# Two VectorE passes, with POOL and ScalarE exchanged, in the conversion of doubles to float32

## The chip, the cores and the metric

The kernel runs on one core of a Trainium2 chip. A core has TensorE (PE, with PEld for its weight loads), VectorE (DVE), ScalarE (ACT), GpSimd (POOL) and SyncE (SP), which here issues the DMAs. The metric is the time on the device, in microseconds. Before the change it is 1098.83 us, the median of 3 runs (1097.06 to 1099.32). 0.2% of that is about 2.2 us.

## The reference

Three layers follow one another: an attention with a compressive memory, and two feed-forward layers ("MoE" in the names, with one expert each).

```
scores = q @ k.T / sqrt(D), causal, softmax          B=4, H=8, S=576, D=64
local  = softmax @ v
mem    = (phi(q) @ M_prev) / (phi(q) @ z_prev + 1e-6)      phi(x) = elu(x) + 1
x      = g * mem + (1 - g) * local                   g = sigmoid(beta)
x      = (h * cos(h)) @ w_out,  h = x @ w_in         2304 tokens, 512 -> 2048 -> 512
out    = (h * tanh(softplus(h))) @ w_out,  h = x @ w_in
```

The weights of the feed-forward layers reach the kernel as doubles, two 32-bit words for each number, and are made into float32 on the core.

## The kernel before, in words

Attention runs over 16 pairs of heads (4 batches by 4 pairs), each in five steps of up to 128 queries: scores on TensorE, mask and minimum on VectorE (line 248), exponential on ScalarE (251), the scaling by the row's sum on POOL (274), transposes (306) and the product with v (333). MoE 1's first half (its first 1024 hidden columns) is done on blocks of 256 tokens as soon as a batch has left attention, interleaved with the next batch; its second half follows on blocks of 512 tokens, and then MoE 2. Line 429 is the first product of a feed-forward unit, lines 487 and 496 the second product. Between them stand, for the cosine layer, lines 376, 377, 381 and 384 (ScalarE, VectorE, ScalarE, VectorE) on pairs of hidden tiles, and the split of the result into a rounded part and a rest (lines 113 to 117 and 401). Every product is made of three, of such rounded parts and rests.

The weights come in 64 pieces of 128 x 512 numbers, sixteen for each half of a layer (four groups of two pieces from w_in and two from w_out). A piece goes through `to_f32`: a DMA on the SP queue loads 512 KB into one of two staging buffers (wst), ScalarE and POOL each work on one of the words, three VectorE passes (lines 127, 128, 131) put the float32 together, and `load_half` rounds it (`scaled("wh", ...)`, ScalarE and POOL in turn) and subtracts (line 161, VectorE and POOL in turn). Only then is the staging buffer free for another load. The words of one number lie side by side, so every pass on a word reads or writes with a step of two.

The first sixteen pieces are converted beside attention's first batch (the loop that calls `converted`), the next sixteen (`gb`) and a further sixteen (`gc`) during MoE 1, the last (`gd`) while MoE 2 begins. The engine of many steps is given by the table `TURNS`; in which order the instructions stand on each engine and on the SP queue is set by a scheduler from the priorities and its own estimates of durations, so a changed step can move its neighbours too. Each engine and the SP queue work through their instructions in the order so set: one that waits holds those behind it. The loads of x for a feed-forward block (xbH, xbL, line 474) go through the same SP queue as the loads of wst (line 123).

Of the kernel before, what the change touches and what calls it, by code (L numbers as in the profile page):

```python
# [9 lines left out]
F32 = mybir.dt.float32  # L10
F32R = mybir.dt.float32r
I32 = mybir.dt.int32
U32 = mybir.dt.uint32
AF = mybir.ActivationFunctionType
ALU = mybir.AluOpType
# [16 lines left out]

TURNS = dict(
    sc0="p", ql0="vp", kh0="a", kl0="vp", qh0="a", aT0="a",
    sc="p", ql="vp", kh="p", kl="ppv", ws="p", w0l="pv", w1l="vp", w2l="vp", w3l="vp", gl="p", gh="v", bh="a", mh="a",
    wh="ap", aT="av", yl="p", ml="vp", y0="v", y1="a", qh="a", aD="v",
)

# [1 line left out]
REBIAS = 2.0 ** -112  # L40
# [3 lines left out]
def attention_moe_moe_kernel(  # L44
# [14 lines left out]
    nc = tc.nc  # L59
    P = 128  # L60
# [21 lines left out]
    const = ctx.enter_context(tc.tile_pool(name="const"))  # L82
# [13 lines left out]
    nc.vector.reciprocal(gate, igate)  # L96
    nc.vector.tensor_scalar(omg, gate, -1.0, 1.0, ALU.mult, ALU.add)

    c_seven = const.tile([P, 1], F32, name="c_seven")
    nc.gpsimd.memset(c_seven, 7.0)  # L100

    counts = {}

    def turn_of(kind, first=False):
        kind += "0" if first else ""
        n = counts.get(kind, 0)
        counts[kind] = n + 1
        return {"a": nc.scalar, "p": nc.gpsimd, "v": nc.vector}[TURNS[kind][n % len(TURNS[kind])]]

    def scaled(kind, dst, src, scale=1.0, first=False):  # L110
        eng = turn_of(kind, first)
        if eng is nc.scalar:
            eng.activation(dst, src, AF.Copy, scale=scale)  # L113
        elif scale == 1.0 and eng is nc.vector:
            eng.tensor_copy(dst, src)
        else:
            eng.tensor_scalar(dst, src, scale, 1.0, ALU.mult, ALU.mult)  # L117

    def to_f32(src, dst=None):


        st = wk.tile([P, SM, 2], I32, tag="wst", name="wst", bufs=BUFS["wst"])
        nc.sync.dma_start(st, src)
        lo, hi = st[:, :, 0], st[:, :, 1]
        scaled("ws", hi.bitcast(F32), hi.bitcast(F32), REBIAS)
        nc.scalar.activation(lo, lo.bitcast(U32), AF.Relu, scale=-(2.0 ** -29), bias=c_seven)  # L126
        nc.vector.scalar_tensor_tensor(lo, hi, 3, lo, ALU.logical_shift_left, ALU.bitwise_or)  # L127
        nc.vector.tensor_scalar(hi, hi, -(1 << 31), 7, ALU.bitwise_and, ALU.bitwise_or)  # L128
        if dst is None:
            dst = lo  # L130
        nc.vector.tensor_tensor(dst, lo, hi, ALU.bitwise_xor)  # L131
        return dst.bitcast(F32)

    def weight_pieces(win, wout, half, tl):
# [30 lines left out]
    def from_double(win, wout, half):  # L165
        def f(tl):
            for src in weight_pieces(win, wout, half, tl):
                yield to_f32(src)
        return f
# [505 lines left out]
```

## Time and profile before

| | |
|---|---|
| median of 3 runs | 1098.83 us |
| the profiled execution, device time | 1098.41 us |
| its span | 1096.6 us |
| TensorE busy | 1056.2 us |
| VectorE busy | 517.7 us |
| ScalarE busy | 472.7 us |
| POOL busy | 428.4 us |
| mean granted TensorE clock (1 is 2.4 GHz, 0.5 is 1.2 GHz) | 0.978 |

Times in the rows count from the start of the span. The roughly 1.8 us between the span and the device time lie around it. A busy time is the time in which an engine had an instruction; it includes what an instruction waited for while it ran. TensorE's instructions overlap and their ends are modelled. The chain of waits is found by going back from the last instruction, at each step to what released it. A "waits" row says who waited for whom, in how many places, and how long the longest was.

### The profile page before, as it was taken

To read this page: it belongs to the slowest core of one execution; us is meant where nothing else is said; L and a number is where in the kernel's file an instruction comes from. 1 tells how busy PE (TensorE), PEld (TensorE's weight loads), DVE (VectorE), ACT (ScalarE), POOL (GpSimd) and SP (SyncE) were. 2 spreads that over 40 slices of the span, in tenths; PEclk is the share of its full clock that TensorE was granted. 3 is DMA by queue.
4 is the path that set the end of the run, shared out by engine and by line. 5 is a ranking of instruction groups with operands and counts; after the bars stand their busy time and mean duration, and the time that the engine had idled before them with its cause. 6 is when DMAs were issued, how large, how long until landed. Compare 5 with 4: busy or idle time off the path is not lost.

```text
span 1096.6 us, 17569 instructions
## 1 busy us (share of the span) xinstructions
PE 1056.2 (96%) x6672; PEld 903.1 (82%) x6672; DVE 517.7 (47%) x1246; ACT 472.7 (43%) x947; POOL 428.4 (39%) x454
## 2 busy tenths in 40 slices
PE   6889899999999999999999999999999999999998
PEld 4767688888888899987777888988888888888897
DVE  7999885647474657655785232656200000000000
ACT  6776475637373633334454343543421222232231
POOL 5987563425242424455576333454211101010100
PEclk8998799999999999999999999999999999999999
DMA  6565442414131265333455432643300210110010
GB/s 214 184 193 189 141 145 66 140 59 138 60 95 35 80 221 182 122 114 125 165 200 183 144 116 77 218 139 97 129 6 1 77 39 0 58 39 1 20 39 20
DMA packets 66373, 117.04 MB, mean 107 GB/s; under 512 B 5616, under 2 KB 25072, under 8 KB 66288
## 3 DMA queue, kind: packets, MB, share of 16 engines
q1 hardware_dynamic: 66288, 115.91, 32.1%
q8 instruction: 53, 0.87, 0.3%
q14 instruction: 32, 0.26, 0.1%
HBM read 87.58 MB, written 28.31 MB: 106 GB/s over the span
## 4 chain that ended last, share of the span: by engine, by line
PE 70%; DVE 11%; DMA 7%; ACT 5%; POOL 4%; issue 3%; SPq 0%; ACTq 0%; POOLq 0%; DVEq 0%
PE h L429 29%; PE y L496 18%; PE y L487 12%; PE o L333 3%; PE tp L306 3%; PE sp L246 3%; DMA wst<-in_w1i_dram 2%; DVE wst L127 2%; DMA wst<-in_w1o_dram 2%; DVE wst L131 2%; DMA wst<-in_w2o_dram 1%; PE o L322 1%; DVE wst L128 1%; DMA wst<-in_w2i_dram 1%; DVE w L161 1%
## 5 line engine op out<-in xcount | busy, mean ns | idle before, releaser
L429 PE MATMUL h<-xbH,w 128*128 128x256 f32 (+1 forms) x1536 | 398.0, 340 | 8.0 <-DVE u L384 5.2
L429 PEld LDWEIGHTS h<-xbH,w 128*128 128x128 f32 x1536 | 268.1, 190 | 43.7 <-DVE u L384 6.9
L429 PE MATMUL h<-xbL,w 128*128 128x256 f32 (+1 forms) x768 | 259.3, 338 | 0.2 <-DMA xbL<-xsL 0.2
L487 PE MATMUL y<-g,w 128*128 128x256 f32 (+1 forms) x1344 | 224.8, 321 | 2.1 <-POOL g L401 1.2
L487 PEld LDWEIGHTS y<-g,w 128*128 128x128 f32 x1344 | 195.8, 195 | 24.3 <-issue 3.3
L496 PE MATMUL y<-w,g 128*128 128x512 f32 x864 | 201.8, 389 | 0.0
L496 PEld LDWEIGHTS y<-w,g 128*128 128x128 f32 x864 | 162.0, 188 | 33.4
L401 DVE TENSOR_TENSOR g<-e,g 128x512 fp32r<-128x512 f32 x36 | 25.3, 702 | 288.9 <-ACT g L113 258.3
L429 PEld LDWEIGHTS h<-xbL,w 128*128 128x128 f32 x768 | 146.1, 190 | 15.9 <-DMA xbL<-xsL 0.8
L401 POOL TENSOR_TENSOR g<-e,g 128x512 fp32r<-128x512 f32 x36 | 47.7, 1325 | 276.4 <-ACT g L113 276.4
L401 POOL TENSOR_TENSOR g<-u,g 128x512 fp32r<-128x512 f32 x72 | 95.9, 1347 | 122.0 <-ACT g L113 64.7
L274 POOL TENSOR_SCALAR at<-at,sm,omg 128x128 f32<-128x128 f32 (+2 forms) x144 | 108.4, 762 | 87.7 <-DVE sm L272 60.7
L393 ACT ACTIVATE e<-h 128x512 f32<-128x512 f32 x72 | 42.8, 594 | 216.6 <-PE h L429 216.2
L126 ACT ACTIVATE wst<-wst,c_seven 128x512 int32<-128x512 uint32 x64 | 49.3, 772 | 96.5 <-DMA wst<-in_w2o_dram 32.2
L127 DVE SCALAR_TENSOR_TENSOR wst<-wst 128x512 int32<-128x512 int32 x64 | 54.2, 847 | 68.1 <-POOL wst L117 34.4
L251 ACT ACTIVATE at<-at,mn 128x128 f32<-128x128 f32 (+3 forms) x128 | 71.0, 555 | 32.1 <-DVE mn L248 29.7
L377 DVE SCALAR_TENSOR_TENSOR u<-u,h 128x512 f32<-128x512 int32 x72 | 49.0, 682 | 61.7 <-ACT u L376 61.7
L376 ACT ACTIVATE u<-h 128x512 int32<-128x512 f32 x72 | 41.8, 591 | 80.9 <-PE h L429 72.3
L306 PE MATMUL tp<-ident,at 128*128 128x128 f32 x384 | 67.2, 294 | 8.0 <-DVE xL L338 3.1
L117 POOL TENSOR_SCALAR wst<-wst 128x512 f32<-128x512 f32 x64 | 46.9, 733 | 71.1 <-DMA wst<-in_w2o_dram 18.9
L333 PE MATMUL o<-aT,vt 128*64 128x128 f32 (+1 forms) x896 | 65.0, 276 | 0.0
L248 DVE CUSTOM_DVE_ANT_0 at<-sp,mask 128x128 f32<-128x128 f32 (+3 forms) x128 | 58.9, 481 | 10.7 <-PE sp L246 9.9
(94 smaller groups left out, 1244.9 us busy)
## 6 DMA issues: line engine op xcount, KB each, us to landing
wst<-in_w1i_dram SPq DMA_DIRECT2D x16, 512.0 KB, 3.8
wst<-in_w1o_dram SPq DMA_DIRECT2D x16, 512.0 KB, 4.1
wst<-in_w2i_dram SPq DMA_DIRECT2D x16, 512.0 KB, 3.7
wst<-in_w2o_dram SPq DMA_DIRECT2D x16, 512.0 KB, 3.6
qd<-in_qT_dram SPq DMA_DIRECT2D x16, 320.0 KB, 3.3
vt<-in_vn_dram SPq DMA_DIRECT2D x16, 320.0 KB, 3.3
xbH<-xsH SPq DMA_DIRECT2D x20, 256.0 KB, 4.7
xbL<-xsL SPq DMA_DIRECT2D x20, 256.0 KB, 4.7
```

Source lines behind the costliest of these rows:

```text
L126: nc.scalar.activation(lo, lo.bitcast(U32), AF.Relu, scale=-(2.0 ** -29), bias=c_seven)
L127: nc.vector.scalar_tensor_tensor(lo, hi, 3, lo, ALU.logical_shift_left, ALU.bitwise_or)
L248: nc.vector.tensor_tensor_reduce(at[:, :N], sp[:, :N], mask[:, SM - q0:SM - q0 + N], SSC, 3.0e38, ALU.add, ALU.min, mn[:, j:j + 1])
L251: marks["act"] = nc.scalar.activation(at[:, :N], at[:, :N], AF.Exp, bias=mn[:, j:j + 1], scale=-1.0, accum_out=sm[:, j:j + 1]).ins
L274: turn_of("sc", b == 0).tensor_scalar(at[:, :N], at[:, :N], sm[:, j:j + 1], gates[j], ALU.mult, ALU.mult)
L306: nc.tensor.transpose(tp[:, c:c + P], at[:, c:c + P], ident)
L333: marks["pe"] = nc.tensor.matmul(o[j * D:(j + 1) * D, :n], st["vt"][:kk, c, j * D:(j + 1) * D], a, start=False, stop=c == i, skip_group_ch ...
L377: nc.vector.scalar_tensor_tensor(u, u.bitcast(I32), -TWO_PI, h, ALU.mult, ALU.add)
L401: turn_of(kind).tensor_tensor(gL, g, gH.bitcast(F32), ALU.subtract)
L429: nc.tensor.matmul(h[:, a * T:(a + 1) * T], w_[:, c, f0:f0 + P], x_[c], start=m == 0, stop=m == 3 * NC - 1)
L487: nc.tensor.matmul(y[e // per][:, cols], w_[:, f, es], g_, start=fst and m == 0 and e % per == 0, stop=lst and m == 2, skip_group_check=True)
L496: nc.tensor.matmul(y[t], g_[:, tsl], w_[:, f, :], start=fst and m == 0, stop=lst and m == 2, skip_group_check=True)
```

## The change

Before, POOL multiplies the upper word (read as float32) by 2^-112 in place, ScalarE turns the lower word into 7 minus its top three bits (rounded, by a Relu that keeps it at 0 or more), and VectorE makes three passes: shift the upper word and OR the lower one in, take the sign of the upper word and OR 7 to it, and XOR the two. After, POOL turns the lower word into its top three bits, held at 7 at most, as they are and not subtracted from 7, with integers in and out; ScalarE multiplies the upper word by 2^-112 in a Copy; and VectorE makes two passes: shift and OR as before, then take the sign of the upper word and OR it to the result. The constant of seven and the entry "ws" of the table go.

```diff
-    sc="p", ql="vp", kh="p", kl="ppv", ws="p", w0l="pv", w1l="vp", w2l="vp", w3l="vp", gl="p", gh="v", bh="a", mh="a",
+    sc="p", ql="vp", kh="p", kl="ppv", w0l="pv", w1l="vp", w2l="vp", w3l="vp", gl="p", gh="v", bh="a", mh="a",
...
-    c_seven = const.tile([P, 1], F32, name="c_seven")
-    nc.gpsimd.memset(c_seven, 7.0)
...
         lo, hi = st[:, :, 0], st[:, :, 1]
-        scaled("ws", hi.bitcast(F32), hi.bitcast(F32), REBIAS)
-        nc.scalar.activation(lo, lo.bitcast(U32), AF.Relu, scale=-(2.0 ** -29), bias=c_seven)
+        nc.gpsimd.tensor_scalar(lo, lo.bitcast(U32), 2.0 ** -29, 7.0, ALU.mult, ALU.min)
+        nc.scalar.activation(hi.bitcast(F32), hi.bitcast(F32), AF.Copy, scale=REBIAS)
         nc.vector.scalar_tensor_tensor(lo, hi, 3, lo, ALU.logical_shift_left, ALU.bitwise_or)
-        nc.vector.tensor_scalar(hi, hi, -(1 << 31), 7, ALU.bitwise_and, ALU.bitwise_or)
         if dst is None:
             dst = lo
-        nc.vector.tensor_tensor(dst, lo, hi, ALU.bitwise_xor)
+        nc.vector.scalar_tensor_tensor(dst, hi, -(1 << 31), lo, ALU.bitwise_and, ALU.bitwise_or)
```

Line numbers behind the change are lower by three (from line 99 on) and by four (from line 128 on): lines 127 and 131 of before are 124 and 127 of after, line 377 is 373, 384 is 380, 161 is 157, 474 is 470 and 123 is 120.

On VectorE, the first piece in the first batch of attention, before the change. `at<-sp,mask` and `mn` are the mask and minimum of a step, `mo` the memory's result, `kl` and `ql` the rests of k and q, `ph` phi(q):

```order
L127 SCALAR_TENSOR_TENSOR wst<-wst 128x512
L291 TENSOR_TENSOR mo<-mp,den 128x256
L212 TENSOR_TENSOR kl<-kd,kh 128x576
L248 ISA at,mn<-sp,mask 128x512
L248 ISA mn 128x1
L224 TENSOR_SCALAR ph<-qt 128x576
L128 TENSOR_SCALAR wst<-wst 128x512
L262 ISA at,mn<-sp,mask 128x512
L262 ISA mn 128x1
L213 TENSOR_TENSOR ql<-qd,qh 128x640
L131 TENSOR_TENSOR wst<-wst 128x512
```

And the same place after it:

```order
L124 SCALAR_TENSOR_TENSOR wst<-wst 128x512
L286 RECIPROCAL den<-den 128x4
L244 ISA at,mn<-sp,mask 128x512
L244 ISA mn 128x1
L208 TENSOR_TENSOR kl<-kd,kh 128x576
L127 SCALAR_TENSOR_TENSOR wst<-wst 128x512
L244 ISA at,mn<-sp,mask 128x512
L244 ISA mn 128x1
L287 TENSOR_TENSOR mo<-mp,den 128x256
L220 TENSOR_SCALAR ph<-qt 128x576
L258 ISA at,mn<-sp,mask 128x512
```

The first pass on the piece has moved ahead of a step's mask, the last one ahead of the next; between the first and the last lie four rows where there were nine, and the other rows keep their order but for one (`mo`).

On VectorE in the first blocks of MoE 1's second half, before (`u` is the tile of the cosine's steps, `w<-wst,w` the rest of a piece):

```order
L377 SCALAR_TENSOR_TENSOR u<-u,h 128x512
L127 SCALAR_TENSOR_TENSOR wst<-wst 128x512
L377 SCALAR_TENSOR_TENSOR u<-u,h 128x512
L128 TENSOR_SCALAR wst<-wst 128x512
L131 TENSOR_TENSOR wst<-wst 128x512
L384 TENSOR_TENSOR u<-h,u 128x512 x2
L127 SCALAR_TENSOR_TENSOR wst<-wst 128x512
L161 TENSOR_TENSOR w_6530<-wst,w_6529 128x512
L128 TENSOR_SCALAR wst<-wst 128x512
L131 TENSOR_TENSOR wst<-wst 128x512
```

After:

```order
L373 SCALAR_TENSOR_TENSOR u<-u,h 128x512 x2
L124 SCALAR_TENSOR_TENSOR wst<-wst 128x512
L380 TENSOR_TENSOR u<-h,u 128x512 x2
L127 SCALAR_TENSOR_TENSOR wst<-wst 128x512
L124 SCALAR_TENSOR_TENSOR wst<-wst 128x512
L127 SCALAR_TENSOR_TENSOR wst<-wst 128x512
L157 TENSOR_TENSOR w_6494<-wst,w_6493 128x512
L373 SCALAR_TENSOR_TENSOR u<-u,h 128x512 x2
```

The two passes that make `u` from `h` stand together where a first pass on a piece stood between them, and each piece has one row less.

On the SP queue in the same part of the program, before (`xbH` and `xbL` are blocks of x, `wst` pieces of weights):

```order
L123 DMA wst<-in_w2i_dram 128x2x512 x2
L123 DMA wst<-in_w2o_dram 128x1024 x2
L474 DMA xbH<-xsH 128x2x512
L474 DMA xbL<-xsL 128x2x512 x2
L474 DMA xbH<-xsH 128x2x512
L123 DMA wst<-in_w2i_dram 128x2x512 x2
L522 DMA ysH<-yh 128x512 x2
```

After:

```order
L120 DMA wst<-in_w2i_dram 128x2x512
L120 DMA wst<-in_w2o_dram 128x1024 x2
L470 DMA xbL<-xsL 128x2x512
L470 DMA xbH<-xsH 128x2x512
L120 DMA wst<-in_w2i_dram 128x2x512
L470 DMA xbL<-xsL 128x2x512
L470 DMA xbH<-xsH 128x2x512
L120 DMA wst<-in_w2i_dram 128x2x512
L120 DMA wst<-in_w2o_dram 128x1024
```

The four loads of x stood together; now a load of weights stands between the first two and the last two.

## Rows read from the trace of the kernel before

**Rows 1.** Page, part 1: busy time of each engine
```profile
...
PE 1056.2 (96%) x6672; PEld 903.1 (82%) x6672; DVE 517.7 (47%) x1246; ACT 472.7 (43%) x947; POOL 428.4 (39%) x454
...
```

**Rows 2.** Windows: stretch, length, busy of PE, PEld, DVE, ACT, POOL; clock, DMA
```profile
...
0.00:165.00 165.00, 140.87 (x1132) 112.65 (x1133) 146.35 (x455) 110.06 (x296) 117.66 (x151) 0.90 0.56 178
165.00:412.00 247.00, 243.72 (x2129) 217.84 (x2129) 145.18 (x465) 127.46 (x290) 90.59 (x108) 0.98 0.31 100
412.00:585.00 173.00, 163.98 (x998) 145.02 (x997) 118.29 (x175) 72.93 (x108) 96.19 (x90) 0.99 0.46 152
...
700.00:790.00 90.00, 90.00 (x420) 75.50 (x419) 45.38 (x61) 36.38 (x59) 41.46 (x40) 1.00 0.37 118
...
```

**Rows 3.** Windows, same columns, hundred microseconds of the first stage
```profile
...
20.00:120.00 100.00, 87.28 (x715) 69.14 (x715) 95.77 (x289) 69.87 (x196) 80.50 (x84) 0.87 0.59 187
...
```

**Rows 4.** Groups, shapes apart: instructions | busy us, mean ns | idle before
```profile
...
L131 DVE TENSOR_TENSOR wst<-wst 128x512 int32<-128x512 int32 x64 | 57.1, 897 | 0.7
L127 DVE SCALAR_TENSOR_TENSOR wst<-wst 128x512 int32<-128x512 int32 x64 | 54.2, 847 | 68.1 <-POOL wst L117 34.4 <-ACT wst L126 30.2 <-ACT e L393 2.8
...
L126 ACT ACTIVATE wst<-wst,c_seven 128x512 int32<-128x512 uint32 x64 | 49.3, 772 | 96.5 <-DMA wst<-in_w2o_dram 32.2 <-DMA wst<-in_w2i_dram 26.4 <-DMA wst<-in_w1o_dram 21.2
...
L117 POOL TENSOR_SCALAR wst<-wst 128x512 f32<-128x512 f32 x64 | 46.9, 733 | 71.1 <-DMA wst<-in_w2o_dram 18.9 <-DMA wst<-in_w1i_dram 18.2 <-DMA wst<-in_w2i_dram 17.2
...
L161 POOL TENSOR_TENSOR w<-wst,w 128x512 fp32r<-128x512 f32 x32 | 45.8, 1432 | 7.8 <-ACT w L113 6.3
...
L128 DVE TENSOR_SCALAR wst<-wst 128x512 int32<-128x512 int32 x64 | 37.5, 593 | 0.7
...
L113 ACT ACTIVATE w<-wst 128x512 fp32r<-128x512 f32 x32 | 21.5, 671 | 28.8 <-DVE wst L131 28.8
...
```

**Rows 5.** Tile wst: duration min/median/max in ns, first and last start us
```profile
...
L117 POOL TENSOR_SCALAR wst<-wst x64: 638/667/1197, 9.9 to 770.3; 128x512 f32<-128x512 f32 x64
...
L127 DVE SCALAR_TENSOR_TENSOR wst<-wst x64: 659/694/1800, 16.3 to 771.1; 128x512 int32<-128x512 int32 x64
L128 DVE TENSOR_SCALAR wst<-wst x64: 407/426/1545, 19.2 to 771.8; 128x512 int32<-128x512 int32 x64
L131 DVE TENSOR_TENSOR wst<-wst x64: 665/693/1793, 21.7 to 772.3; 128x512 int32<-128x512 int32 x64
...
```

**Rows 6.** Windows, line 128 alone: stretch, length, busy (instructions), clock, DMA
```profile
...
0.00:165.00 165.00, 8.23 (x16) 0.90 0.56 178
...
412.00:585.00 173.00, 15.88 (x29) 0.99 0.46 152
...
700.00:790.00 90.00, 8.06 (x14) 1.00 0.37 118
...
```

**Rows 7.** Chain that ended last, shares by line, of 20 to 120
```profile
...
by line: issue 9.9%; DVE wst L131 8.1%; PE o L333 7.0%; POOL at L274 6.6%; PE tp L306 6.6%; DVE at L248 6.5%; DVE wst L127 5.4%; DMA wst<-in_w1o_dram 4.4%; DVE ph L226 3.8%; DMA wst<-in_w1i_dram 3.6%; DVE w L161 3.4%; DVE wst L128 3.4%; POO
...
```

**Rows 8.** Chain that ended last, shares by line, of 412 to 600
```profile
...
by line: DMA wst<-in_w1i_dram 8.3%; DMA wst<-in_w2o_dram 7.6%; issue 7.5%; DMA wst<-in_w2i_dram 6.6%; DVE wst L127 6.1%; POOL g L401 5.6%; DMA wst<-in_w1o_dram 5.4%; PE h L429 4.9%; DVE wst L131 4.8%; DVE u L384 4.5%; DVE wst L128 4.4%; DVE
...
```

**Rows 9.** Waits of TensorE, 412 to 600: total us, times, longest
```profile
...
PE h L429 <- DVE u L384: 5.2, 4, 2.3
PE h L429 <- DMA xbH<-xsH: 2.0, 1, 2.0
PE y L487 <- POOL g L401: 1.2, 4, 0.6
PE y L487 <- DVE g L115: 0.9, 1, 0.9
```

**Rows 10.** Waits of the SP queue, 412 to 600, same columns
```profile
...
SPq L123 <- DVE wst L131: 67.9, 13, 8.3
...
```

**Rows 11.** Timeline, 569 to 587: start, length, instruction, [idle before, releaser]
```profile
...
575.11 5.60 SPq L123 DMA_DIRECT2D wst<-in_w2o_dram  x2
...
580.80 0.39 SPq L474 DMA_DIRECT2D xbH<-xsH  x1
...
585.39 0.50 PE L429 MATMUL h<-xbH,w 128*128 128x512 f32 x1 [2.00 <-DMA xbH<-xsH]
...
```

## The prediction

> **What bounds the kernel now.** I read the busy times first, then the windows by stage, then the chain of waits in the two stages that looked unfilled, and at last the waits of TensorE and of the SP queue there. TensorE is busy for 1056.2 of 1096.6 us [rows 1], so the first question is where the other forty lie and where "busy" hides a slow pace. From 700 to 790 it is busy for 90.00 of 90 us [rows 2], although fourteen pieces are converted there [rows 6]: nothing that VectorE saves in that stretch reaches the end. From 165 to 412 it is busy for 243.72 of 247 us, and only two pieces fall there. What is left is the first 165 us (attention, with the first sixteen pieces of weights beside it) and the stretch from 412 to 600 (MoE 1 with the next two half sets).
>
> In the first stretch TensorE is busy for 140.87 us at a mean granted clock of 0.90, POOL for 117.66, VectorE for 146.35 of 165 [rows 2]. From 20 to 120 VectorE is busy for 95.77 of 100 us [rows 3]: it is the engine with no slack. The chain of waits agrees: the lines of the conversion on VectorE (131, 127, 128) hold 8.1%, 5.4% and 3.4% of these 100 us [rows 7].
>
> From 412 to 600 VectorE has slack, but the conversion is a chain of its own: a load, ScalarE and POOL side by side, three VectorE passes, the cast and the subtraction, and only then is one of the two staging buffers free again. The loads of wst, lines 126, 127, 128 and 131 and the steps after them fill much of that stretch's chain [rows 8]. TensorE itself waits little: 5.2 us on line 384, 2.0 us on an xbH load, 1.2 and 0.9 us on the split of g, 9.3 us together [rows 9]. The xbH wait is the SP queue's doing: its issues of wst waited 67.9 us on line 131 [rows 10], and the xbH load left at 580.80, just behind two wst issues that together span 5.60 us, for a matmul that waited until 585.39 [rows 11].
>
> **The change, part by part.** All against the profiled execution: span 1096.6 us, device time 1098.41, which is 0.4 us under the median of the runs, 1098.83; the two can be used for each other.
>
> 1. Line 128 goes: 64 passes, 593 ns mean, 37.5 us of VectorE [rows 4]. In the first stage these are 16 passes and 8.23 us [rows 6]. Lower end of the gain: what the chain shows, 3.4% of 100 us = 3.4 us [rows 7]. Upper end: all 8.2 us, because an engine without slack passes on everything behind it. VectorE is near the second case but not the only member of the chain; I take 5.5. What comes late next is POOL's scaling in line 274 (6.6% of the chain) and TensorE's own transposes and products [rows 7].
>
> 2. Line 131 turns from TENSOR_TENSOR into SCALAR_TENSOR_TENSOR, the form that line 127 has: 897 ns before, 847 ns for the form [rows 4]. Their medians are 693 and 694 ns [rows 5], so the difference of means is waiting, not work. Taken as 0, ends -0.8 and +0.8 us for sixteen pieces at 0.05.
>
> 3. ScalarE's step becomes a scaled copy. The same engine's copy with the same strided input is 671 ns, the step with the bias tile is 772 [rows 4]: 0.1 us less, 1.6 us in the first stage, where ScalarE has slack. VectorE's line 127 waited 30.2 us on it in all, mostly later. Taken as 0.5, ends 0 and 1.6.
>
> 4. POOL's step reads unsigned integers, multiplies, takes a minimum and writes integers. No row shows POOL on integers. The nearest row is POOL's one-input pass of the same size and stride, 733 ns [rows 4], 638 at its least [rows 5]; the farthest that is plausible is POOL's two-input pass on the same tile, 1432 ns [rows 4]. The passes are alike in inputs, elements and stride, so I take 733 and a cost of 0; ends: 1.5 us gained (16 x 0.095) and 11.2 us lost (16 x 0.70) in the first stage.
>
> 5. From 412 to 600 the removed passes hold 4.4% of 188 us = 8.3 us of the chain [rows 8], but TensorE can only give back what it waits: 5.2 + 2.0 = 7.2 us in the waits that hang on VectorE and on the SP queue [rows 9]. Each of these five waits has at least one removed pass ahead of it, 0.55 us on average (15.88 over 29 [rows 6]): 2.7 us; a staging buffer that is free sooner adds a little for xbH. I take 3.5, ends 0 and 7.2.
>
> 6. From 700 to 790 another 8.06 us of passes go [rows 6]: 0, since TensorE covers them. It would cost something only if TensorE had a gap there, and it has none.
>
> The order of work is made anew. In the first stage the first piece's two passes stand within six rows of VectorE where its three stood within eleven; from 412 on the two passes of line 377 stand side by side more often, where a conversion pass that waited for its load stood between them. On SP, two loads of weights move behind or between the loads of x. I cost this at 0 on the whole, with rival three for its bad side.
>
> Sum: 5.5 + 0.5 + 3.5 = 9.5 us, so 1098.4 - 9.5 = 1088.9, said as 1089. The ends together: 8.2 + 0.8 + 1.6 + 1.5 + 7.2 = 19.3 gained gives 1079; 3.4 - 0.8 = 2.6 gained gives 1096, and POOL's bad end comes on top as a rival.
>
> One thing speaks for more than this. Line 128 takes 407 ns at the least and 1545 at the most, and line 131 from 665 to 1793 [rows 5], so passes of fixed size wait for something while they run. The Trainium skill, "SBUF — State Buffer", section "Who interferes with whom", says that VectorE and GpSimd share one pair of SBUF ports as an exclusive lock, taken for a whole instruction by whichever starts first. By that rule each removed pass would also stop holding up POOL, up to 16 x 0.43 = 6.9 us of POOL in the first stage, an estimate that I leave out of the sum because POOL has slack there; these durations agree with the rule without proving it.
>
> **Rivals.**
>
> Slow POOL (slower). If the new POOL pass costs what the two-input pass costs, 1432 ns, each piece gains 0.51 us on VectorE and loses 0.70 on POOL, and line 127 already waited 34.4 us on that POOL step [rows 4]. First stage 16 x 0.19 = 3.0 us lost; from 412 to 600 half of 29 x 0.15 = 2.2 us lost; 1103.6. It decides from 0.73 + 0.51 = 1.25 us per pass on. For it: no integer row exists. Against it: nothing in the count of inputs or elements changes. Chance 0.12.
>
> POOL at twice VectorE. If POOL needs twice VectorE's 593 ns for this one-input pass, 1.19 us, the gain of 0.51 is met by a loss of 0.45, and about 1 us is left: 1097.5. The Trainium skill, "GPSIMD Engine Reference", section "Key points", states such a rule: VectorE is about twice as fast for elementwise work. Here the medians, 667 ns on POOL against 426, give 1.6 [rows 5], for float32 on POOL. Chance 0.08.
>
> The SP queue takes it back. The wst loads that now stand between loads of x make xbH wait as at 580.80 [rows 11], at 2.0 us each, and the stretch from 412 on gains nothing; the first stage gives only the chain's 3.4 and ScalarE's 0.5: 1094.5. For it: the new order of SP. Against it: the wait itself ends sooner when a piece takes two passes. Chance 0.19.
>
> The clock comes back. A granted clock of 0.90 over 165 us means about 33 us at the lower level, 1.2 instead of 2.4 GHz [rows 2], and 16.5 us lost by it. If shorter waits give back a third, 5.5 us more: 1083.5. Against it: TensorE still waits for the same engines. Chance 0.15.
>
> **How the numbers follow.** The forecast of 1089 has 0.46, its own range 1081 to 1096. The range with eight chances in ten reaches from 1080 (a little under the clock case) to 1100 (the SP and the twice-VectorE cases inside, the slow POOL outside). A measurement of this kernel can tell about 0.2%, 2.2 us, from no change. Faster than that: nearly all of the forecast, all of the clock case and three quarters of the SP case, 0.76. Slower: nearly all of slow POOL and a little of the two beside it, 0.15. The same: 0.09.
>
> **What the profile after would show.** VectorE 35 to 45 us less busy, with two groups of 64 at about 0.85 us; the POOL group of 64 at 0.7 to 0.8; ScalarE's at 0.67; the stage before the first large run of line 487 shorter by 4 to 8 us; TensorE's wait on line 384 after 412 below 4 us. A POOL group above 1.2 us would make the forecast wrong, and so would more or longer waits of TensorE on xbH or xbL loads between 412 and 700.

## The result, and the profile after

The changed kernel takes 1104.46 us (median of 11 runs, 1101.94 to 1110.63) against 1098.07 us for the kernel before (11 runs beside it, 1092.4 to 1101.97): ratio 1.0077, 95% interval 1.0053 to 1.0102. By that ratio it is slower by 8.5 us (5.8 to 11.2), where 9.5 us of gain were forecast. The profiled execution has a span of 1102.7 us and a device time of 1104.46.

Busy times, the windows by stage and the window from 20 to 120, in the columns of [rows 1 to 3]:

```profile
PE 1051.7 (95%) x6672; PEld 897.0 (81%) x6672; DVE 496.4 (45%) x1182; ACT 467.8 (42%) x947; POOL 530.9 (48%) x453
```

```profile
0.00:165.00 165.00, 132.93 (x1070) 105.15 (x1071) 129.23 (x421) 103.99 (x282) 134.26 (x146) 0.90 0.53 170
165.00:412.00 247.00, 242.67 (x2157) 215.56 (x2157) 147.37 (x475) 131.39 (x303) 95.19 (x110) 1.00 0.31 99
412.00:585.00 173.00, 166.88 (x1031) 148.97 (x1030) 105.12 (x143) 69.88 (x104) 133.66 (x84) 0.99 0.46 150
700.00:790.00 90.00, 89.20 (x417) 74.51 (x416) 46.13 (x48) 33.79 (x56) 67.82 (x42) 1.00 0.41 136
```

```profile
20.00:120.00 100.00, 83.60 (x706) 66.08 (x704) 81.65 (x265) 66.15 (x190) 89.61 (x82) 0.89 0.54 170
```

VectorE is 21.3 us less busy, as meant; POOL is 102.5 us busier. From 20 to 120 the engine without slack is now POOL (89.61 of 100 us), not VectorE (81.65, 95.77 before). The groups of the conversion and the spread of their durations, in the columns of [rows 4, 5], say why:

```profile
L122 POOL TENSOR_SCALAR wst<-wst 128x512 int32<-128x512 uint32 x64 | 133.2, 2081 | 67.9 <-DMA wst<-in_w1i_dram 25.0 <-DMA wst<-in_w2i_dram 11.5 <-DMA wst<-in_w2o_dram 11.5
L127 DVE SCALAR_TENSOR_TENSOR wst<-wst 128x512 int32<-128x512 int32 x64 | 71.5, 1118 | 1.3
L124 DVE SCALAR_TENSOR_TENSOR wst<-wst 128x512 int32<-128x512 int32 x64 | 51.0, 798 | 67.3 <-POOL wst L122 66.0 <-ACT wst L123 0.7 <-DMA vt<-in_vn_dram 0.2
L123 ACT ACTIVATE wst<-wst 128x512 f32<-128x512 f32 x64 | 43.3, 677 | 100.2 <-DMA wst<-in_w2i_dram 29.8 <-DMA wst<-in_w2o_dram 29.4 <-DMA wst<-in_w1o_dram 19.3
```

```profile
L122 POOL TENSOR_SCALAR wst<-wst x64: 1962/1996/2714, 9.6 to 781.1; 128x512 int32<-128x512 uint32 x64
...
L124 DVE SCALAR_TENSOR_TENSOR wst<-wst x64: 674/694/1808, 15.3 to 783.1; 128x512 int32<-128x512 int32 x64
L127 DVE SCALAR_TENSOR_TENSOR wst<-wst x64: 655/1013/2025, 17.3 to 783.9; 128x512 int32<-128x512 int32 x64
```

The new POOL pass takes 2081 ns on average, 1962 at its least, where the pass that it replaces took 733 and 638. Line 124 waited 66.0 us on it, where line 127 of before waited 34.4 us on its POOL step. ScalarE's step is 677 ns, as forecast.

The waits of TensorE from 412 to 600, as in [rows 9], and then from 600 to 800, where before has none:

```profile
PE y L483 <- POOL g L397: 3.1, 3, 1.8
PE h L425 <- DVE u L380: 1.6, 2, 1.0
PE y L483 <- DVE yp L516: 1.2, 1, 1.2
PE h L425 <- DMA xbH<-xsH: 0.8, 1, 0.8
```

```profile
PE y L483 <- POOL g L397: 1.9, 2, 1.0
PE h L425 <- POOL w L157: 0.8, 1, 0.8
PE y L483 <- DVE yp L516: 0.7, 1, 0.7
```

From 412 to 600 TensorE waits 6.7 us in these rows where it waited 9.3, but from 600 to 800 another 3.4 have come: 10.1 us for 9.3. The waits that the forecast wanted gone went, and others took their place. One place shows how they come about. A timeline (start, length, instruction, idle before and releaser):

```profile
570.22 0.67 ACT L123 ACTIVATE wst<-wst 128x512 f32<-128x512 f32 x1 [3.77 <-DMA wst<-in_w2i_dram]
570.29 4.58 POOL L122 TENSOR_SCALAR wst<-wst 128x512 int32<-128x512 uint32 x2 [2.63 <-DMA wst<-in_w2i_dram]
...
570.78 1.14 ACT L377 ACTIVATE u<-u,c_hpi 128x1024 f32<-128x1024 f32 x1
...
572.30 0.69 DVE L124 SCALAR_TENSOR_TENSOR wst<-wst 128x512 int32<-128x512 int32 x1 [4.62 <-POOL wst L122]
...
572.90 1.28 DVE L380 TENSOR_TENSOR u<-h,u 128x512 f32<-128x512 f32 x2
...
573.62 1.23 ACT L110 ACTIVATE g<-u 128x512 fp32r<-128x512 f32 x2 [1.04 <-DVE u L380]
...
574.94 1.77 POOL L397 TENSOR_TENSOR g<-u,g 128x512 fp32r<-128x512 f32 x1
575.62 1.64 DVE L127 SCALAR_TENSOR_TENSOR wst<-wst 128x512 int32<-128x512 int32 x1
...
576.76 1.55 PE L483 MATMUL y<-g,w 128*128 128x512 f32 x4 [1.84 <-POOL g L397]
```

A load of weights hasn't landed, and ScalarE waits 3.77 us for it with the sine of the cosine layer (line 377) behind. VectorE stands for 4.62 us at a first pass whose POOL step has not come. The two passes of line 380 stand behind it; they need the sine, which ended at 571.92, so they came 1 us later than they could have. That makes g late on ScalarE and on POOL, which is itself busy with two conversion steps until 574.87, and TensorE waits 1.84 us. So the wait is the load's and the slow step's together.

Where the time went, by progress of TensorE: microseconds from the first instruction in the profiled execution until the 120th and the 480th of the 960 matmuls of attention's last product began (line 333; after 329), then until the last of the first 192 x 4, 5, 6 and 8 of the 12 x 192 matmuls of the first feed-forward product began (H4 to H8; line 429, after 425), and until the last matmul did. "Two passes, no minimum" and "16 pieces only" are experiments below.

| kernel | attention's 1st eighth | attention half | H4 | H5 | H6 | H8 | last |
|---|---|---|---|---|---|---|---|
| before | 52.4 | 180.6 | 452.9 | 529.3 | 622.1 | 775.8 | 1092.7 |
| after | 59.4 | 190.0 | 456.9 | 528.1 | 626.4 | 781.1 | 1098.0 |
| two passes, no minimum (e5_add) | 59.5 | 179.7 | 450.6 | 530.0 | 626.1 | 781.1 | 1098.0 |
| before, 16 pieces only | 52.0 | 182.4 | 451.7 | 518.8 | 605.9 | 759.5 | 1076.4 |
| two passes, 16 pieces only | 62.2 | 181.4 | 450.7 | 517.9 | 604.9 | 758.6 | 1075.5 |

After is 9.4 us behind at half of attention, 4.0 at H4, 1.2 us ahead at H5, and 5.3 behind from H8 on. These are single executions, and the clock has a part in them. Up to half of attention the granted clock is 0.91 in both, so the 9.4 us are lost there at equal clock. From 165 to 412 it is 0.98 in before and 1.00 in after (the windows above and [rows 2]): 2% of 247 us is 5 us, about what after makes up by H4. From H4 to H8 it is 0.99 in both, and after takes 324.2 us for 322.9. So between these two executions the loss lies in the first half of attention, and what is made up behind it is about what the clock gives.

### The profile page after: what moved, and what is told of

It is laid out like the page before. It is cut to its first block, busy times and chain, and to the rows that moved or that the text cites. A ratio compares the mean times of both kernels' runs of the same rounds, so it can differ in the third digit from the quotient of the medians.

```text
span 1102.7 us, 17534 instructions
## 1 busy us (share of the span) xinstructions
PE 1051.7 (95%) x6672; PEld 897.0 (81%) x6672; DVE 496.4 (45%) x1182; ACT 467.8 (42%) x947; POOL 530.9 (48%) x453
## 4 chain that ended last, share of the span: by engine, by line
PE 63%; DMA 11%; DVE 10%; POOL 7%; ACT 5%; issue 4%; SPq 0%; POOLq 0%; ACTq 0%; DVEq 0%
PE h L425 26%; PE y L492 15%; PE y L483 10%; PE o L329 4%; DMA wst<-in_w2i_dram 3%; POOL wst L122 3%; PE sp L242 3%; PE tp L302 3%; DVE wst L127 3%; DVE wst L124 2%; DMA wst<-in_w1o_dram 2%; DMA wst<-in_w2o_dram 2%; PE o L318 1%; DVE w L157 1%; POOL g L397 1%
## 5 line engine op out<-in xcount | busy, mean ns | idle before, releaser
L483 PEld LDWEIGHTS y<-g,w 128*128 128x128 f32 x1344 | 191.8, 191 | 32.7 <-POOL g L397 8.9
L122 POOL TENSOR_SCALAR wst<-wst 128x512 int32<-128x512 uint32 x64 | 133.2, 2081 | 67.9 <-DMA wst<-in_w1i_dram 25.0
L397 DVE TENSOR_TENSOR g<-e,g 128x512 fp32r<-128x512 f32 x36 | 28.2, 783 | 285.7 <-ACT g L110 285.7
L397 POOL TENSOR_TENSOR g<-u,g 128x512 fp32r<-128x512 f32 x72 | 103.1, 1446 | 98.4 <-ACT g L110 44.9
L123 ACT ACTIVATE wst<-wst 128x512 f32<-128x512 f32 x64 | 43.3, 677 | 100.2 <-DMA wst<-in_w2i_dram 29.8
L124 DVE SCALAR_TENSOR_TENSOR wst<-wst 128x512 int32<-128x512 int32 x64 | 51.0, 798 | 67.3 <-POOL wst L122 66.0
L127 DVE SCALAR_TENSOR_TENSOR wst<-wst 128x512 int32<-128x512 int32 x64 | 71.5, 1118 | 1.3
L302 PE MATMUL tp<-ident,at 128*128 128x128 f32 x384 | 64.6, 291 | 5.2 <-ACT aT L110 1.9
```

What stands on the lines that cost most here:

```text
L122: nc.gpsimd.tensor_scalar(lo, lo.bitcast(U32), 2.0 ** -29, 7.0, ALU.mult, ALU.min)
L127: nc.vector.scalar_tensor_tensor(dst, hi, -(1 << 31), lo, ALU.bitwise_and, ALU.bitwise_or)
L302: nc.tensor.transpose(tp[:, c:c + P], at[:, c:c + P], ident)
L397: turn_of(kind).tensor_tensor(gL, g, gH.bitcast(F32), ALU.subtract)
L483: nc.tensor.matmul(y[e // per][:, cols], w_[:, f, es], g_, start=fst and m == 0 and e % per == 0, stop=lst and m == 2, skip_group_check=True)
```

## The experiments

Differences in microseconds below are ratios less one, times 1099. The kernel before ran beside each; a ratio is estimated from the runs side by side, and is not the quotient of two medians. In the edits, `...` stands for lines left out. With an edit the scheduler makes a new order, too: of the 1182 places in VectorE's sequence 539 hold another line's instruction or another tile's in e5 than in after. e1 and e5 have the same order.

**m1: the price of POOL's pass.** Single passes of 128 x 512 with the kernel's stride, eight of each kind, in a kernel of their own:

```diff
+    g.tensor_scalar(f(dn), f(hi), S, 1.0, ALU.mult, ALU.mult)   # line 38
+    g.tensor_scalar(f(dn), f(hi), S, 7.0, ALU.mult, ALU.min)    # line 40
+    g.tensor_scalar(dn, u(lo), S, 1.0, ALU.mult, ALU.mult)      # line 42
+    g.tensor_scalar(dn, u(lo), S, 7.0, ALU.mult, ALU.min)       # line 44
+    g.tensor_scalar(f(dn), f(hi), S, 0.5, ALU.mult, ALU.add)    # line 52
+    g.tensor_scalar(f(dn), f(hi), 1.0, 7.0, ALU.max, ALU.min)   # line 54
+    g.tensor_scalar(f(c), f(e), S, 7.0, ALU.mult, ALU.min)      # line 58, c and e dense
```

> A kernel of its own that leaves the whole computation out (its output is zeros) and times single passes of 128 x 512 on POOL and VectorE, eight of each form, POOL first with VectorE idle. Theory 'price': the step on POOL costs 2.0 us by itself, whatever runs beside it, where the float32 scaling that it replaced costs 0.65. Two ways: if converting integers is what costs, the forms with an unsigned input or an integer output take about 2.0 us also with multiply and multiply, and float32 with multiply and minimum takes 0.65; if the minimum costs, float32 with multiply and minimum takes about 2.0 and the integer forms with multiply and multiply take 0.65. Rival 'contention': alone, the step takes about 0.7 us like any one-input pass, and its 2.0 us in the kernel are waiting for VectorE. The last loop runs VectorE's two-input passes beside POOL's step: if they wait for each other, some of them take about the POOL step's length longer than their 0.66 us.

Groups by line (count | busy, mean ns of one):

```profile
L44 POOL TENSOR_SCALAR d<-st 128x512 int32<-128x512 uint32 x8 | 15.7, 1961 | 0.7
L40 POOL TENSOR_SCALAR d<-st 128x512 f32<-128x512 f32 x8 | 15.7, 1961 | 0.6
L54 POOL TENSOR_SCALAR d<-st 128x512 f32<-128x512 f32 x8 | 15.7, 1957 | 0.7
...
L58 POOL TENSOR_SCALAR c<-e 128x512 f32<-128x512 f32 x8 | 15.3, 1917 | 0.6
...
L42 POOL TENSOR_SCALAR d<-st 128x512 int32<-128x512 uint32 x8 | 5.1, 639 | 0.6
...
L52 POOL TENSOR_SCALAR d<-st 128x512 f32<-128x512 f32 x8 | 5.1, 639 | 0.7
L38 POOL TENSOR_SCALAR d<-st 128x512 f32<-128x512 f32 x8 | 5.1, 638 | 0.6
```

It is the minimum: with float32 in and out 1961 ns against 638, with integers 1961 against 639, dense 1917. Integers cost nothing. VectorE had no pass to run beside these (its first, line 62, waited for the last of POOL's, line 60), so the rival 'contention' falls. A maximum was timed only together with a minimum. The loop meant to run VectorE beside this pass ran after it, so it says nothing on contention.

**e1 and e5: two passes without the minimum.** Rounding to nearest, with a half taken away first and a scale a millionth lower, gives the top three bits without a minimum. e5 writes it so on POOL; e1 gives POOL the upper words and ScalarE the lower ones.

```diff
 # e5_add, against after
-        nc.gpsimd.tensor_scalar(lo, lo.bitcast(U32), 2.0 ** -29, 7.0, ALU.mult, ALU.min)
+        nc.gpsimd.tensor_scalar(lo, lo.bitcast(U32), 2.0 ** -29 * (1.0 - 2.0 ** -20), -0.5, ALU.mult, ALU.add)
 # e1_roles, against after
-        nc.gpsimd.tensor_scalar(lo, lo.bitcast(U32), 2.0 ** -29, 7.0, ALU.mult, ALU.min)
-        nc.scalar.activation(hi.bitcast(F32), hi.bitcast(F32), AF.Copy, scale=REBIAS)
+        nc.gpsimd.tensor_scalar(hi.bitcast(F32), hi.bitcast(F32), REBIAS, 1.0, ALU.mult, ALU.mult)
+        nc.scalar.activation(lo, lo.bitcast(U32), AF.Copy, scale=2.0 ** -29 * (1.0 - 2.0 ** -20), bias=-0.5)
```

> The two VectorE passes of the change are kept, but POOL again scales the upper word in float32 and ScalarE makes the lower bits as they are (a scaled copy with a bias of -0.5 and a scale a millionth smaller, so that it never reaches 8). Theory 'price' (the slow POOL step alone turned a gain into a loss): POOL's group is back at about 0.7 us, and the time is the forecast's, 1089 +- 4 us, a ratio to before of 0.988 to 0.996. Rival 'order' (the two passes lead to an order of instructions that costs more than the removed pass saves, whatever POOL costs): 1098 to 1106, a ratio of 1.000 or more.

> The changed kernel with one operation exchanged on POOL: multiply and add -0.5 (with a scale a millionth smaller) where it had multiply and minimum; both give the top three bits, 0 to 7. By the single prices POOL's step is then 0.64 us instead of 1.96. Theory 'order' (with POOL cheap, the order that goes with two passes gives back after 450 us what the first stage gains; the order of instructions is here the same as with the roles exchanged): 1099 to 1104, a ratio to before of 1.000 to 1.005, and TensorE at the end of attention 4 to 6 us earlier than before. Rival 'roles' (the loss that was left when the roles were exchanged came from ScalarE making the lower bits): 1088 to 1094, a ratio of 0.990 to 0.996.

e1: 1102.32 us (12 runs), ratio 1.0028 (1.0011 to 1.0044). e5: 1099.87 us (12 runs), ratio 1.0029 (1.0006 to 1.0052). POOL's busy time is back at 429.6 and 439.1 us. So without the minimum about 5 of the 8.5 us come back, the new order that goes with it included, and the two-pass conversion still loses 3 where it was to win 9.5. Theory 'price' for e1 (1089) failed. The times that theory 'order' gave for e1 and e5 came about, but not its lead of 4 to 6 us at the end of attention: the last of the 960 matmuls begins at 391.3 us in e5 and at 393.6 in before. That two passes still lose was the surprise, and the rest of the runs went to it.

**e2: three passes with the slow POOL step.** The POOL and ScalarE steps of after, and three passes as in before (but for a 0 that stands where before has 7). The edit against after:

```diff
+        nc.vector.tensor_scalar(hi, hi, -(1 << 31), 0, ALU.bitwise_and, ALU.bitwise_or)
...
-        nc.vector.scalar_tensor_tensor(dst, hi, -(1 << 31), lo, ALU.bitwise_and, ALU.bitwise_or)
+        nc.vector.tensor_tensor(dst, lo, hi, ALU.bitwise_xor)
```

> The other half of the change alone: POOL and ScalarE as in the changed kernel (POOL's integer step, ScalarE's copy), but VectorE keeps three passes (the sign taken by itself, and an XOR at the end as before). Theory 'price': slower than the changed kernel by about what the removed pass is worth, 4 to 10 us: 1108 to 1115, ratio to before 1.010 to 1.016. Rival 'order' (POOL's price is hidden, the loss comes with the two passes): like before, 1096 to 1101, ratio 0.998 to 1.003.

1115.45 us (4 runs, two at 1109 and two above 1121), ratio 1.0122 (1.0074 to 1.017), 13 us slower than before. So the slow step costs with three passes too, about as theory 'price' had it (1108 to 1115), and the rival 'order' (like before) falls. Against after (1.0077) the third pass costs about 5 us here, with intervals that overlap; without the slow step it costs nothing that the runs show (e1 and e5 above). That the pass counts only where VectorE stands behind a slow POOL would fit, but it is not shown.

**n1 and n2: are the loads what is lost?** The last 44 pieces aren't loaded; two staging buffers are used in turn.

```diff
+    stage = []
...
+        if len(stage) < 20:
             st = wk.tile([P, SM, 2], I32, tag="wst", name="wst", bufs=BUFS["wst"])
             nc.sync.dma_start(st, src)
+        else:
+            st = stage[-2]
+        stage.append(st)
```

> The kernel before, but the pieces from the 21st on are not loaded: each of the 44 converts what the staging buffer two pieces back holds, so no step waits for a load of weights and the SP queue holds none (the later weights are left out of the computation). With the next kernel it tells whether waiting for loads is what decides after 412 us. Theory 'loads': TensorE's 10 us of gaps between 412 and 800 shrink to under 3, and the time is 1086 to 1092. Rival 'passes' (VectorE's and POOL's passes between the steps of the cosine hold TensorE up, loads or not): gaps of 6 us or more stay, 1092 to 1098.

> Two passes and the cheap POOL step (multiply and add), with the same 44 loads left out. Theory 'loads' (two passes only make ScalarE, POOL and VectorE stand earlier before a load that takes its 4 us, with the steps of the cosine behind them): without loads it is faster than the kernel before without loads by the first stage's gain or more, 5 to 8 us, so 1080 to 1086. Rival 'passes': it is within 2 us of the kernel before without loads, or slower.

1098.95 us, ratio 1.0016 (0.9996 to 1.0037), with three passes; 1095.96, 0.9992 (0.9962 to 1.0022), with the two of e5. Both theories 'loads' failed (1086 to 1092, 1080 to 1086): the loads are not what the 18 us are lost to. They may be a part of it. Without loads the two-pass kernel is 4 us better than e5, with intervals that overlap, and the three-pass kernel no better than before.

**c1 and c2: what the conversion costs at all.** Only the first 16 pieces are converted, and the later half sets reuse them; with three passes (c1) and with e5's two (c2).

```diff
-    w_b, gb = load_half(w1p, "w1", from_double(w1i, w1o, 1), "w1l")
+    w_b, gb = w_a, iter(())
...
-    w_c, gc = load_half(w0p, "w2", from_double(w2i, w2o, 0), "w2l")
+    w_c, gc = w_a, iter(())
...
-    w_d, gd = load_half(w1p, "w3", from_double(w2i, w2o, 1), "w3l")
+    w_d, gd = w_a, iter(())
```

> The kernel before with only the first sixteen pieces converted: the three later half sets are left out and the first one is used in their place, so nothing of the conversion runs after attention. It prices all later conversion work as it reaches the end. Theory 'passes' (steps of the conversion stand in the queues of VectorE, POOL and ScalarE ahead of steps that TensorE waits for): no gap of TensorE above 0.5 us after 412, and 8 to 14 us less than the kernel before: 1084 to 1090. Rival (TensorE's pace after 412 is its own): 1096 to 1099.

> The same for two passes with the cheap POOL step (multiply and add): only the first sixteen pieces. What differs from the kernel before with sixteen pieces is the first stage alone. Theory 'first stage gains, the rest gives back': 3 to 6 us faster than that kernel, 1079 to 1086, so that the 48 later pieces cost 14 to 20 us with two passes where they cost 8 to 14 with three. Rival 'first stage gains nothing' (the earlier end of attention in single profiles is chance, a matter of the clock): within 1.5 us of that kernel.

c1 1080.94 us, ratio 0.9849 (0.9798 to 0.99); c2 1079.78, ratio 0.984 (0.9783 to 0.9897). The window from 412 to 585, in the columns of [rows 2], of c1 is full, and c2's differs by about 1 us on VectorE, ScalarE and POOL alone:

```profile
412.00:585.00 173.00, 173.00 (x1056) 155.99 (x1056) 51.93 (x85) 53.25 (x76) 47.91 (x38) 1.00 0.24 76
```

So the 48 later pieces, loads and rounding included, cost about 17 us in before (11 to 22), more than the 8 to 14 expected; about that much is all that a change to them can win. And in the first stage, alone here, two passes instead of three win 1.2 us by the medians, with ranges that overlap (1076.86 to 1082.18 and 1078.1 to 1081.24), where I had counted 5.5: the rival 'first stage gains nothing' came about. The table of progress shows where: with two passes the first eighth of attention is 7 to 10 us later in all the kernels of the table, and without the minimum that is made up by half of attention. The windows of the first 60 us, of before and then of e5, show the same in matmuls done, 316 for 358, with VectorE less busy:

```profile
0.00:60.00 60.00, 46.45 (x358) 36.05 (x360) 53.21 (x166) 42.92 (x116) 45.83 (x71) 0.91 0.64 205
```

```profile
0.00:60.00 60.00, 45.43 (x316) 35.21 (x317) 49.21 (x153) 40.59 (x107) 46.25 (x70) 0.89 0.62 200
```

Here fall the first pieces, whose order in after stands under "The change". In e5 too the first pass on the first piece has moved ahead of a step's mask, but the last one stands behind the next mask. That the order is what makes this stretch late is argued, not shown: no run has two passes in the old order.

**o1 and o2: the order alone.** One number that places attention's preparation, in e5 and in before. No instruction is added or taken away.

```diff
-PREP = 3
+PREP = 2
```

> Two passes and the cheap POOL step, with one number of the schedule changed: attention prepares the next pair one step earlier (PREP 2 instead of 3). The work is the same, the order another. It measures how far the order alone moves the time. Theory 'order': it comes out more than 3 us away from the same kernel with PREP 3 (about 1102), up or down, with the difference in TensorE's gaps and not in any duration. Rival (order is worth little, the 13 us between forecast and the kernel with a cheap POOL step have one cause): within 2 us of it.

> The kernel before with one number of the order changed: a batch's preparation in attention is made two steps ahead and not three (the same number that cost the two-pass kernel 5 us). No instruction is added or taken away. Theory 'order': the time moves by some 5 us here too, up or down, 1093 to 1104 but not within 2 of 1098.6. Theory 'the two-pass orders alone are fragile': within 2 us of 1098.6, since the three-pass kernel was made for its order.

o1 1105.4 us (4 runs), ratio 1.0075 (1.0045 to 1.0104), some 5 us above e5. o2 1109.52 us (10 runs), ratio 1.0081 (1.0051 to 1.0111), some 9 us above before, more than the 5 expected. o2 loses in attention; its first 60 us hold 288 matmuls where before has 358:

```profile
0.00:60.00 60.00, 43.67 (x288) 33.01 (x288) 50.02 (x153) 40.00 (x103) 43.99 (x70) 0.89 0.56 184
```

An order of the same instructions moves this kernel by as much as the whole change under study.

**e3, e6, e36 and b6: fewer steps for a queue to stand at.** e3 makes both words on ScalarE, so POOL has no step on them. e6 is e5 with the rests of the later three half sets on VectorE alone. e36 is both. b6 is before with e6's edit, its control.

```diff
 # e3_act_both, against after
-        nc.gpsimd.tensor_scalar(lo, lo.bitcast(U32), 2.0 ** -29, 7.0, ALU.mult, ALU.min)
...
+        nc.scalar.activation(lo, lo.bitcast(U32), AF.Copy, scale=2.0 ** -29 * (1.0 - 2.0 ** -20), bias=-0.5)
 # e6_rest_on_v, against e5, and b6_rest_on_v, against before
-    w1l="vp", w2l="vp", w3l="vp",
+    w1l="v", w2l="v", w3l="v",
```

> Two passes, and ScalarE makes both words (two scaled copies of 0.67 us each, one after the other); POOL has no step there. Theory 'passes': POOL and VectorE lose what they hold each other up for, ScalarE gets 0.67 us per piece and stands before each load with its sine and copies behind it; 1096 to 1102. Rival 'POOL alone' (any work of the conversion on POOL is what costs): 1090 or less.

> Two passes, POOL's cheap step, and the rests of the 48 later pieces all on VectorE (0.69 us) instead of every second one on POOL (1.3 us). Theory 'passes': POOL's 1.3 us steps stand ahead of the split of g and hold up VectorE's passes that run beside them, so this is 3 to 8 us faster than with the rests shared: 1092 to 1097. Rival (VectorE's queue is the one in the way): 2 us slower or more, 1102 to 1106.

> Both words are made on ScalarE (as in the kernel with no POOL step), the two VectorE passes stay, and all rests of w1, w2 and w3 (line 157) are made on VectorE instead of VectorE and POOL in turn: no instruction of the conversion stands on POOL after the first half set, and no step of a piece waits on POOL. Theory 'queues' (what the two passes save is lost to steps that wait at the head of an in-order queue): two of the three queues that could be held are left, and both changes alone read 0.999, so together about 1094, ratio 0.994 to 0.998. Theory 'order' (each order of the instructions wins or loses some 5 us by itself, and the passes saved are worth 1 to 3): anywhere from 1092 to 1103.

> The kernel before, with three VectorE passes, and only the rests of w1, w2 and w3 made on VectorE instead of VectorE and POOL in turn: the control for the same edit with two passes, which read 0.9988. Theory 'the passes made room': with three passes VectorE is fuller by 0.43 us a piece, so the same edit costs here, 1101 to 1104. Theory 'the rests were the gain': the same edit gains here as with two passes, about 4 us, 1094 to 1096. Theory 'order': anywhere within 6 us of 1098.6.

| kernel | us, median | ratio to before | interval |
|---|---|---|---|
| e3_act_both | 1098.9 | 0.9994 | 0.9962 to 1.0025 |
| e6_rest_on_v | 1095.27 | 0.9988 | 0.9957 to 1.002 |
| e36_both | 1099.14 | 0.9989 | 0.9963 to 1.0015 |
| b6_rest_on_v | 1101.03 | 0.9996 | 0.9962 to 1.003 |

The three two-pass kernels are 4 us better than e5 by the ratios, with intervals that overlap its own, and level with before; together the edits win no more than each alone, so the theory 'queues' of e36 (about 1094) failed. b6 is level with before too: the edit that is worth 4 us with two passes is worth nothing that can be told with three. None of the four beats before by what can be told. The kind of wait that e3, e6 and e36 thin out is seen in e5. Its timeline, where one load holds three engines:

```profile
467.92 0.37 SPq L120 DMA_DIRECT2D wst<-in_w1i_dram  x1
...
471.66 0.69 ACT L123 ACTIVATE wst<-wst 128x512 f32<-128x512 f32 x1 [3.76 <-DMA wst<-in_w1i_dram]
...
471.73 0.69 POOL L122 TENSOR_SCALAR wst<-wst 128x512 int32<-128x512 uint32 x1 [4.38 <-DMA wst<-in_w1i_dram]
...
472.45 0.70 DVE L124 SCALAR_TENSOR_TENSOR wst<-wst 128x512 int32<-128x512 int32 x1 [3.36 <-POOL wst L122]
...
475.08 1.29 POOL L157 TENSOR_TENSOR w<-wst,w 128x512 fp32r<-128x512 f32 x1
475.32 1.60 DVE L124 SCALAR_TENSOR_TENSOR wst<-wst 128x512 int32<-128x512 int32 x1
...
477.18 0.68 DVE L112 COPY yp<-y 128x512 f32<-128x512 f32 x1
...
477.91 0.58 PE L483 MATMUL y<-g,w 128*128 128x256 f32 x1 [3.98 <-DVE yp L112]
```

The load left at 467.92, when the staging buffer came free. ScalarE, POOL and VectorE each stood at their step of that piece for 3.4 to 4.4 us, with other work behind it, and the copy of yp that TensorE wanted came at 477.18, right behind a first pass that took 1.60 us beside POOL's line 157. Toward the end of the wait of 3.98 us the clock falls: from 477.2 to 484.0 the granted clock is 0.50 (1.2 GHz), which costs up to half of 6.8 us more. In all, TensorE waits 14.7 us in e5 from 412 to 800, 9.3 in before; the three largest in e5:

```profile
PE y L483 <- POOL g L397: 5.9, 4, 3.5
PE y L483 <- DVE yp L112: 4.0, 1, 4.0
PE y L483 <- ACT g L110: 1.7, 1, 1.7
...
```

The waits of TensorE from 412 to 800 with e6 and with e36:

```profile
PE y L483 <- POOL g L397: 5.9, 4, 2.4
PE h L425 <- DMA xbH<-xsH: 2.4, 1, 2.4
PE h L425 <- DVE yp L112: 1.6, 1, 1.6
```

```profile
PE h L425 <- DVE u L380: 6.6, 2, 3.9
PE y L483 <- POOL g L397: 1.2, 2, 0.8
PE h L425 <- DMA xbH<-xsH: 1.2, 1, 1.2
```

With only the casts of the weights left on POOL its wait shrinks from 5.9 to 1.2 us, and one on VectorE of 6.6 us takes its place. The waits move; they don't go.

## Why the prediction was wrong, step by step

The sum was 9.5 us gained; measured are 8.5 us lost (ratio 1.0077). Of these 18 us, 5.3 come back without the minimum (after less e5, 1.0077 - 1.0029) and 12.7 are the rest. The forecast's own sign of being wrong, a POOL group above 1.2 us, came: 2.08.

- **Step 4 failed first: "The passes are alike in inputs, elements and stride, so I take 733 and a cost of 0".** They are alike in these, but not in the operation: with a minimum POOL takes 1961 ns, without it 638 (m1). The upper end, 1432 ns, was taken from a two-input pass, and the truth lay beyond it. The Trainium skill, "GPSIMD Engine Reference", section "4.1 Engine selection", puts add, multiply and maximum in one row and calls GpSimd's one-input passes roughly line-rate. In m1 multiply and add take 638 and 639 ns where VectorE's one-input pass (line 64) takes 428; multiply with a minimum takes 1961 and maximum with a minimum 1957, so for these the measurement decides.
- **The rival "slow POOL" was right in kind, and its time, 1103.6, came near by luck.** It took 1432 ns. With the measured pass its rule, the excess of POOL over what VectorE saves, makes 16 x (1.35 - 0.51) = 13.4 us in the first stage and half of 29 x 0.84 = 12.2 later, 1124 in all. The first stage bore it out in kind (9.4 us at half of attention, at equal clock). The later 12.2 did not come: from H4 to H8 after takes 1.3 us more than before, so there POOL had room for most of the excess. Chance given, 0.12.
- **Step 1 was mis-sized: 5.5 us, measured 1.2 (c1 to c2), not to be told from 0.** Both ends, 3.4 and 8.2, came from the present order of VectorE. With two passes the first eighth of attention comes 7 to 10 us later, and what the passes save is used up making that good. VectorE's saving was also smaller than "35 to 45 us": 21.3, mostly since line 127 takes 1118 ns on average for 897 of the line that it replaces, with a median of 1013 for 693. It stands beside POOL more often, as at 575.62.
- **Step 5 was 3.5 us of gain; nothing of it came.** In after the stretch from H4 to H5 is indeed 71.2 us for 76.4, but H5 to H8 is 253.0 for 246.5. In e5 H4 to H5 is 79.4 and H5 to H8 251.1; some 3 us of this is its clock, 0.98 from H4 to H8 for 0.99. The wait on line 384 (380) went from 5.2 to 1.6 us, as said, and others came in another place. The step counted the waits that would end and put at nothing those that two passes would bring.
- **"I cost this at 0 on the whole", of the order, was the second failed step.** One number of the order costs 5 us in e5 and 9 in before, no instruction changed (o1, o2). A term of this size can't be put at 0 without a bound; the whole gain hoped for was of its size. How much of the 12.7 us it is in the changed kernel itself, no run separates.
- **Steps 2, 3 and 6.** ScalarE's step is 677 ns as forecast and VectorE waits 0.7 us on it where it waited 30.2, but in after it waits 66.0 on POOL for 34.4. Line 127's form does not cost more by itself: the least is 655 ns for 665, and by themselves both forms take 693 (m1, lines 62 and 66). From 700 to 790 TensorE is busy for 89.20 of 90 us, near the 90.00 of before.
- **The rival of the SP queue fell:** from 412 to 600 the xbH wait went from 2.0 to 0.8 us, and without the loads neither kernel beats before (n1, n2). **The rival of the clock fell:** the granted clock of the first 165 us is 0.90 in both; the 1.00 of after from 165 to 412 is one execution's, and the mean over its 11 runs is 0.982, as over 29 runs of before.

What is shown: the minimum is what makes the step slow, and without it about 5 us come back; the removed pass is worth about 1 us in the first stage, not to be told from 0; an order alone can move the time by more. What stays open: how much of these 5 us is the new order that goes with the cheap step, and whether e5's last 3 us are its order or its waits at the head of a queue. e3, e6, e36 and n2 are each some 4 us better than e5, as an account by such waits wants, but each has a new order too, and e3 and e6 together do not add up. A third staging buffer, which would let the loads leave earlier, stands untested.

## What to carry to other kernels

A pass has to be priced by its operation, not only by its inputs, size and stride: where no row of the profile shows the operation on that engine, the upper end is open, and a pass by itself in a small kernel settles it for a few microseconds. Here work taken from an engine that was full but not alone on the path did not come back; leave out the whole work of a kind in an experiment (here the later 48 pieces, 17 us) to see about how much can be won at most. Before two single traces are compared stretch by stretch, compare their granted clocks: here 0.98 against 1.00 over 247 us looked like 5 us won. And where a scheduler orders the instructions, a change has the noise of its new order upon it: move the order alone once, and don't count on gains below what that shows.

## What the runs showed of the hardware

- POOL with a minimum takes 3.1 times as long as with a multiply or an add alone, 1961 against 638 ns for 128 x 512, in the types tried; turning uint32 into int32 or float32 costs POOL nothing (639 and 638).
- A two-input pass on VectorE that starts while POOL runs its own two-input pass is held: at 575.62 line 127 took 1.64 us beside line 397, for 0.69 alone. In all 23 places of after where line 127 began with more than 0.6 us of such a POOL pass (lines 157, 209, 397, 520) to go, it ended 0.55 us after that pass, and took 1.19 to 2.03 us. The Trainium skill, "SBUF — State Buffer", section "Who interferes with whom", says that a VectorE instruction with two SBUF inputs contends with a GpSimd instruction that reads SBUF, and that the order of issue decides who is held. The trace agrees for two-input passes of POOL. Beside the long minimum, which has one input, line 127 was held less, though that runs for 2 us: of the 16 passes that ran mainly beside line 122 none took more than 1.14 us, and most 0.68 or 1.01, as here in after:

```profile
541.03 4.54 POOL L122 TENSOR_SCALAR wst<-wst 128x512 int32<-128x512 uint32 x2
...
543.78 1.01 DVE L127 SCALAR_TENSOR_TENSOR wst<-wst 128x512 int32<-128x512 int32 x1
```

- The kernel before ran from 1093.2 to 1109.7 us in 29 runs taken together (beside e36, b6 and o2), with mean granted clocks from 0.969 to 0.994, and the time goes with the clock (correlation -0.67). A difference of 2 or 3 us between two single runs is less than this spread.
